# A key of its own for one memset, and one SBUF copy moved ahead of a weight load, in a fused attention + SwiGLU layer

## The chip, the cores and the metric

The kernel runs on one NeuronCore of one Trainium2 chip. Five instruction streams run side by side and meet only through semaphores: TensorE (PE in the profile, with its weight loads listed apart as PEld), VectorE (DVE), ScalarE (ACT), GpSimd (POOL) and SyncE (SP). SP does no arithmetic here; it issues DMAs, in order, and an instruction that waits holds back all that stands behind it on the same engine. The metric is the device time of one execution in microseconds (us), as the median of several; lower is better. Before the change the median of 3 executions is 597.41 us (596.99 to 597.79).

## The reference

One transformer layer in the parallel form: attention and MLP both read the same normalized input and are summed with the residual. S = 2048 tokens, D = 576, 32 heads of 18, a sliding window of 256 tokens, F = 4608, bfloat16.

```
xn  = layernorm(x)
q, k, v = split(xn @ wqkv)                          # 32 heads of 18
p   = softmax(mask(q k^T * 18^-0.5))                # key within the last 256 tokens
h   = silu(xn @ w1) * (xn @ w3)
out = x + concat_heads(p v) @ wo + h @ w2
```

## The kernel before

The tokens are worked in four chunks of 512 (`NC`, four blocks of 128 tokens each, `TB`). For each chunk the kernel needs the normalized input transposed (`xnT`, features on the partitions, 576 features padded to five blocks of 128), then q and k ("QK tiles", nine matmul groups of five), then v, then 36 MLP units (`NF`), between which the attention scores, exponentials and p v products of that chunk are threaded, and last the output projection (`p2_list`), beside which the QK and v tiles of the next chunk are computed. So chunk 0 alone has a prologue in which nothing of the MLP runs; the change lies there.

**Order and waits.** The program is a flat list. Each `add(engine, ..., r=, w=, j=)` appends one instruction to its engine and names keys: `r` reads a key, `w` starts a new generation of it, and `j` joins the writers of the present generation. A reader depends on every writer that the key has *at the moment the reader is added*. `resolve` (line 99) turns the dependencies into semaphore waits and leaves out those that the engine already knows to be met, directly or through another wait. Nothing reorders the list afterwards: the order in which the Python code calls `add` is the order on each engine.

**The prologue, in the order of the code.**

- Four blocks of x are loaded (`load_x`), then the v columns of wqkv into `wa` (lines 681 to 684), key `("wv", n)`.
- The five blocks of 128 features need 640 rows, wqkv has 576. So rows 64 to 127 of the last block of `wa` are cleared by DVE (line 687); this clear starts the key `wz`. Every matmul that reads `wa` reads `wz` too.
- Ten matmuls on zeros (`warm`, line 691).
- SP issues the q and k columns of wqkv (lines 696 and 697, key `wqk`) and then two sets of MLP weights: `load_w13()` twice. One call loads 512 columns of w3 and of w1 into one of three buffers `w13_0`, `w13_1`, `w13_2`, as two DMAs of 576 KB (line 286). A set serves four MLP units.
- For each block: statistics (DVE), rstd (POOL), normalize (DVE), transpose (PE, line 337), copy to `xnT` (ACT, line 331); and one block later its v matmuls (line 371) and their copies (ACT, line 380).
- `xn_swap(0, "sp")` issues two DMAs of 256 KB (line 344) that copy `xnT` into `xnS` with the two halves of the partitions exchanged. The MLP units use the array as two row halves of 64, and `xnS` gives each half the other half's features. The first of the two waits for all of `xnT`. Every MLP unit reads `xnS` as one key.
- ACT gathers the rest of the QK weights into `w8` (line 727).
- POOL clears the q and k buffers `qk`: slots 0 and 1 (line 731), slot 2 (`clear(2)`, line 711), then the padded rows of `wo` (line 733), then slot 3 (`clear(3)`, line 711). The clear of `wo` is added with `j=["wz"]`: it becomes one more writer of the key that the QK weights read.
- `qk_atoms(0, issue_first)` adds the nine QK tiles (line 360, copied to `stage` by DVE, line 364). The first matmul reads `wqk`, `wz` and all of `xnT`. When the tiles of a head group are done, `repack` issues the DMAs (line 414) that spread `stage` into `qk`: groups 0 and 1 right away on SP, the others held back and issued between the MLP units.
- `load_w13()` for the third buffer, then the first of the held groups.

Then the MLP units of chunk 0 begin (line 607, `unit_pairs`): unit 0 reads `xnS` and `w13_0`, unit 1 ends with the first attention scores (line 468), which need group 0 in `qk`, and unit 4 is the first to read `w13_1`.

The output projection reads `wo` in `p2_item` (line 663) with `r=[("oT", tt), "wo", "wz"]`, for the first time at 144.6 us of the profiled execution.

Of the kernel before, what the change touches and what calls it, by code (L numbers as in the profile page):

```python
# [5 lines left out]
dt = mybir.dt  # L6
# [38 lines left out]
class _Prog:  # L45
# [13 lines left out]
    def add(self, eng, fn, r=(), w=(), j=(), dma=None, after=()):  # L59
        deps = []  # L60
        for k in r:
            deps += self.bufs[k].writers
        for k in w:
            g = self.bufs.get(k)
            if g is not None:
                deps += g.ahead(eng)
        for k in j:
            g = self.bufs[k].before
            if g is not None:
                deps += g.ahead(eng)  # L70
        op = _Op(eng, fn, deps + list(after), dma)
        op.after = tuple(after)
        self.n[eng] += 1
        op.pos = self.n[eng]
        if dma is not None:
            self.dma_count[dma] = self.dma_count.get(dma, 0) + 16
            op.cnt = self.dma_count[dma]
        for k in r:
            self.bufs[k].readers.append(op)
        for k in w:  # L80
            self.bufs[k] = _Gen([op], self.bufs.get(k))
        for k in j:
            self.bufs[k].writers.append(op)
        for k in w:
            if self.bufs[k].before is not None:
                self.bufs[k].before.before = None
        self.ops.append(op)
        return op
# [76 lines left out]
def bass_parallel_sum__sliding_block__glu_gated_swiglu__prompt_kernel(  # L165
# [30 lines left out]
    add = P.add  # L196

    with ExitStack() as es:

        def sb(name, shape, dtype=dt.bfloat16):  # L200
            return es.enter_context(nc.sbuf_tensor(name, shape, dtype))
# [14 lines left out]
        wo = sb("wo", [128, 5, D])  # L216
# [22 lines left out]
        oT = sb("oT", [128, TB, 5, 128])  # L239
# [38 lines left out]
        def load_w13():  # L278
            nonlocal nfill
            if nfill >= NC * NFC:  # L280
                return
            s = nfill % NW13
            c0 = (nfill % NFC) * 512
            nfill += 1
            for n, src in enumerate((B_w3, B_w1)):
                add("sp", lambda e, n=n, src=src: e.dma_start(
                    w13[s][64 * n:64 * n + 64, :, :], src[:, c0:c0 + 512].rearrange("(kd p) f -> p kd f", p=64)),
                    dma=f"w13_{s}", **{"j" if n else "w": [("w13", s)]})
# [3 lines left out]
        def load_w2():  # L292
            nonlocal n2fill
            if n2fill >= NC * 2 * NFC:
                return
            s = n2fill % NW2
            half, fc = divmod(n2fill % (2 * NFC), NFC)
            n2fill += 1
            add("sp", lambda e: e.dma_start(
                w2[s][:], B_w2[fc * 512:(fc + 1) * 512, half * HD:(half + 1) * HD].rearrange("(fl p) d -> p fl d", p=128)),  # L300
                w=[("w2", s)], dma=f"w2_{s}")
# [39 lines left out]
        def xn_swap(c, eng):  # L341
            for n in range(2):
                p, q = 64 * n, 64 - 64 * n
                add(eng, lambda e, p=p, q=q: e.dma_start(
                    xnS[p:p + 64, :, :], xnT[q:q + 64, c % 2, 0:4, :]),
                    r=xk(c), dma="xnS", **{"j" if n else "w": ["xnS"]})

        def xk(c):
            return [("xnT", c % 2, tt) for tt in range(TB)]
# [16 lines left out]
        def v_half(c, tt, half, evac):  # L366
            b = ring()
            slot = (c * TB + tt) % (2 * TB)
            c0 = 2 * D + half * HD
            for kd in range(5):  # L370
                add("pe", lambda e, kd=kd: e.matmul(  # L371
                    PS[:, b, 0:HD], xnT[:, c % 2, kd, tt * 128:(tt + 1) * 128], wa[:, kd, c0:c0 + HD],
                    start=(kd == 0), stop=(kd == 4)),
                    r=[("wv", half), "wz", ("xnT", c % 2, tt)], **{"w" if kd == 0 else "j": [("ps", b)]})
            vv = va[:, slot, :, :].rearrange("p g (hh c) -> p (g hh) c", c=VW)
            dst = vv[:, 16 * half:16 * half + 16, 0:Dh]
            src = PS[:, b, 0:HD].rearrange("p (h d) -> p h d", d=Dh)
            kw = {"w" if half == 0 else "j": [("va", slot)]}
            if evac == "act":
                add("act", lambda e: e.activation(dst, src, ACT.Copy), r=[("ps", b)], **kw)  # L380
            else:
                add("dve", lambda e: e.tensor_copy(dst, src), r=[("ps", b)], **kw)
# [266 lines left out]
        def p2_item(c, item, xs):  # L649
            nonlocal of_ctr  # L650
            what, half, fc, k, tt, sl, last = item
            d0 = half * HD
            bank = PS[:, ACC[tt], 0:HD]
            key = [("ps", ACC[tt])]
            if what == "w2":
                f = fc * 4 + k
                add("pe", lambda e: e.matmul(  # L657
                    bank, hT[:, f, tt * 128:(tt + 1) * 128], w2[sl][:, k, :], start=(f == 0), stop=False),
                    r=[("h", f), ("w2", sl)], **{"w" if f == 0 else "j": key})
                if last:  # L660
                    load_w2()
            elif what == "wo":
                add("pe", lambda e: e.matmul(  # L663
                    bank, oT[:, tt, k, :], wo[:, k, d0:d0 + HD], start=False, stop=(k == 4)),
                    r=[("oT", tt), "wo", "wz"], j=key)
            else:
                o = of_ctr % NOF
                of_ctr += 1
                t = c * TB + tt
                add("dve", lambda e: e.tensor_tensor(ofin[o][:], bank, xp[xs[tt]][:, d0:d0 + HD], ALU.add),  # L670
                    r=key + [("xp", xs[tt])], w=[("of", o)])
                add("sp", lambda e: e.dma_start(out2[t * 128:(t + 1) * 128, d0:d0 + HD], ofin[o][:]),
                    r=[("of", o)], dma=f"out{o}")
# [5 lines left out]
        for n, eng in enumerate(("sp", "act")):  # L679
# [3 lines left out]
                w=[("wv", n)], dma=f"wv{n}")  # L683
# [13 lines left out]
        add("sp", lambda e: e.dma_start(  # L697
            wa[:, 0:4, 0:2 * D], A_wqkv[0:512, 0:2 * D].rearrange("(kd p) f -> p kd f", p=128)), j=["wqk"], dma="wqk")
        load_w13()
        load_w13()  # L700

        vall = va[:, :, :, :].rearrange("p t g (hh c) -> p (t g hh) c", c=VW)
        add("pool", lambda e: e.memset(vall[:, :, Dh:VW], 0.0), w=[("va", i) for i in range(2 * TB)])
# [2 lines left out]
        def first_v(tt):  # L706
            v_half(0, tt, 0, "act")
            v_half(0, tt, 1, "act")

        def clear(slot, keys):  # L710
            add("pool", lambda e: e.memset(qk[:, slot, :, :].bitcast(dt.float32), 0.0), w=keys)
# [3 lines left out]
        for i in range(TB):  # L715
# [7 lines left out]
            if i:  # L723
                first_v(i - 1)
        xn_swap(0, "sp")
        first_v(TB - 1)
        add("act", lambda e: e.activation(
            w8[:, :, :].rearrange("p k (s f) -> p k s f", s=2),
            wa[:, :, 0:2 * D].rearrange("p k (s f) -> p k s f", s=2)[:, :, :, 512:576], ACT.Copy),
            r=["wqk", "wz"], w=["w8"])  # L730
        add("pool", lambda e: e.memset(qk[:, 0:2, :, :].bitcast(dt.float32), 0.0), r=[("xn", 1)], w=[("q", g) for g in range(G)])
        clear(2, [("k", g, 0) for g in range(G)])
        add("pool", lambda e: e.memset(wo[0:64, 4, :].bitcast(dt.float32), 0.0), j=["wz"])
        clear(3, [("k", g, 1) for g in range(G)])

        held = []
# [12 lines left out]
        for c in range(NC):  # L749
# [84 lines left out]
            for n, item in enumerate(p2_list(c)):  # L834
                p2_item(c, item, xs)
                if n in late:
                    what, g = late[n]
                    if what == "pv":
                        pv(c, g, ring())
                        pv_out(g)  # L840
                    else:
                        heads_back(g, ring())
                        heads_out(g)
                elif n in ot_at:
                    o_trans(ot_at[n])
                elif n % 8 == 4 and n > 24:
                    next(proj, None)
# [33 lines left out]
```

## Time and profile before

| | us |
|---|---|
| median of 3 executions | 597.41 (596.99 to 597.79) |
| the profiled execution: its own time | 598.63 |
| the profiled execution: span from the first to the last instruction | 596.9 |
| PE busy | 588.9 (99% of the span) |
| DVE / ACT / POOL busy | 327.7 / 264.8 / 170.1 |
| mean granted TensorE clock over the span | 0.997 |

The busy share of an engine counts the time in which it has an instruction under way; for PE this is no measure of how well the array is used. Times of day below ("at 16.43") are microseconds from the start of the span. The timeline gives for each row the start, the time from the first start to the last end, the engine (SPq is SP's issuing of DMAs), the line, the operation, the tiles written and read, the shape and the count; a bracket tells the idle time of the engine before it and what ended it. The chain of waits is the path that ended last, followed back from the last instruction; "issue" in it is time in which the engine waited for nothing that the profile can name. The busy table by stretches gives busy time and count of instructions of each engine, the clock granted to TensorE (1.00 is full), the share of the DMA engines' time in use (it can be read a little above 1), and their rate in GB/s.

### The profile page before, as it was taken

What the parts mean: (1) busy time and instruction counts of PE and PEld (TensorE: products, weight loads), DVE (VectorE), ACT (ScalarE), POOL (GpSimd) and SP (SyncE); (2) the same over time, 40 slices, a digit from 0 to 9 for tenths busy, and PEclk for the clock granted to TensorE, in tenths of its full rate; (3) what the DMA queues carried; (4) which work ended last, traced back from release to release, by engine and by line L of the source; (5) the groups of instructions that cost most, each with busy time, mean ns of one, the idle gap of its engine ahead of it and who ended that gap; (6) DMA issues with size and microseconds to landing.
All of it is one profiled execution on the core that took longest, in us unless ns stands there. A gap on an engine that the chain in (4) does not pass through costs nothing.

```text
span 596.9 us, 14277 instructions
## 1 busy us (share of the span) xinstructions
PE 588.9 (99%) x6300; PEld 373.1 (63%) x6310; DVE 327.7 (55%) x586; ACT 264.8 (44%) x278; POOL 170.1 (28%) x285
## 2 busy tenths in 40 slices
PE   7899999999999999999999999999999999999998
PEld 4355566667765566566775555656677555555776
DVE  4467887644037778654404778765430566666311
ACT  5066666400038687730005778681000677787000
POOL 6133444200015455420002545441000344444000
PEclk9899999999999999999999999999999999999999
DMA  9798989674536757686462858588446366550452
GB/s 238 149 180 167 193 169 195 136 164 126 149 108 124 137 117 134 150 154 147 112 171 75 161 99 154 96 184 161 122 122 168 81 115 128 113 121 1 102 150 68
DMA packets 99041, 81.17 MB, mean 136 GB/s; under 512 B 5028, under 2 KB 97892, under 8 KB 98980
## 3 DMA queue, kind: packets, MB, share of 16 engines
q1 hardware_dynamic: 93065, 74.53, 58.3%
q10 hardware_dynamic: 5915, 5.74, 4.0%
q8 instruction: 49, 0.80, 0.6%
q14 instruction: 12, 0.10, 0.1%
HBM read 71.07 MB, written 2.36 MB: 123 GB/s over the span
## 4 chain that ended last, share of the span: by engine, by line
PE 98%; DVE 1%; issue 1%; DMA 0%; POOL 0%
PE ps L607 48%; PE ps L657 24%; PE ps L360 7%; PE ps L468 6%; PE ps L514 4%; PE ps L663 3%; PE ps L371 3%; PE ps L540 1%; PE ps L589 1%; DMA xp<-in_A_x_dram 0%; DVE xn L319 0%; PE ps L337 0%; PE ps L591 0%; PE ps L530 0%; DVE stats L307 0%
## 5 line engine op out<-in xcount | busy, mean ns | idle before, releaser
L607 PE MATMUL ps<-xnT,w 64*128 64x512 bf16 x1440 | 218.6, 376 | 0.0
L615 ACT ACTIVATE th<-ps 128x512 bf16<-128x512 f32 x144 | 86.0, 597 | 259.2 <-PE ps L607 259.2
L495 POOL TENSOR_SCALAR_AFFINE_SELECT pt<-pt 128x512 bf16<-128x512 bf16 x174 | 107.4, 643 | 186.7 <-ACT pt L484 186.7
L657 PE MATMUL ps<-w,hT 128*128 128x288 bf16 x1152 | 157.7, 286 | 0.0
L607 PE MATMUL ps<-xnS,w 64*128 64x512 bf16 x1152 | 154.1, 376 | 0.0
L621 DVE SCALAR_TENSOR_TENSOR gs<-th,ps 128x512 bf16<-128x512 bf16 x144 | 98.7, 685 | 95.6 <-ACT th L615 95.5
L657 PEld LDWEIGHTS ps<-w,hT 128*128 128x128 bf16 x1152 | 111.9, 98 | 34.8 <-issue 2.3
L484 ACT ACTIVATE pt<-ps 128x1536 bf16<-128x1536 f32 x87 | 126.2, 1451 | 15.2 <-PE ps L468 13.8
L607 PEld LDWEIGHTS ps<-xnT,w 64*128 64x128 bf16 x1440 | 88.2, 94 | 40.2 <-issue 3.3
L624 DVE SCALAR_TENSOR_TENSOR hT<-gs,ps 128x512 bf16<-128x512 bf16 x144 | 98.9, 687 | 5.0
L607 PEld LDWEIGHTS ps<-xnS,w 64*128 64x128 bf16 x1152 | 66.7, 94 | 54.2
L468 PE MATMUL ps<-qk 64*128 64x128 bf16 (+2 forms) x888 | 88.6, 250 | 0.0
L495 POOL TENSOR_SCALAR_AFFINE_SELECT stage<-stage 128x512 bf16<-128x512 bf16 x66 | 40.5, 639 | 155.8 <-ACT stage L484 155.8
L468 PEld LDWEIGHTS ps<-qk 64*128 64x128 bf16 x888 | 48.5, 94 | 31.7 <-ACT pt L484 14.4
L670 DVE TENSOR_TENSOR ofin<-ps,xp 128x288 bf16<-128x288 f32 x32 | 14.6, 456 | 81.8 <-PE ps L663 81.7
L484 ACT ACTIVATE stage<-ps 128x1536 bf16<-128x1536 f32 x33 | 47.9, 1451 | 5.6 <-PE ps L468 5.1
L364 DVE CAST stage<-ps 128x512 bf16<-128x512 f32 x36 | 24.9, 691 | 38.7 <-PE ps L360 38.7
L360 PE MATMUL ps<-xnT,wa 128*128 128x512 bf16 x150 | 39.1, 393 | 3.1 <-issue 2.6
L360 PEld LDWEIGHTS ps<-xnT,wa 128*128 128x128 bf16 x160 | 16.0, 101 | 17.8 <-issue 5.0
L663 PE MATMUL ps<-wo,oT 128*128 128x288 bf16 x160 | 25.3, 286 | 0.0
L523 DVE CAST uT<-ps 128x512 bf16<-128x512 f32 x32 | 21.9, 683 | 5.0 <-PE ps L514 5.0
L371 PE MATMUL ps<-wa,xnT 128*128 128x288 bf16 x160 | 24.0, 286 | 0.0
(51 smaller groups left out, 260.2 us busy)
## 6 DMA issues: line engine op xcount, KB each, us to landing
w<-in_B_w_dram SPq DMA_DIRECT2D x72, 576.0 KB, 7.8
w<-in_B_w_dram SPq DMA_DIRECT2D x72, 288.0 KB, 3.2
xp<-in_A_x_dram SPq DMA_DIRECT2D x30, 144.0 KB, 7.2
qk<-stage ACTq DMA_DIRECT2D x75, 36.0 KB
out_dram<-ofin SPq DMA_DIRECT2D x32, 72.0 KB, 1.8
xnS<-xnT ACTq DMA_DIRECT2D x6, 256.0 KB, 5.4
wa<-in_A_wqkv_dram SPq DMA_DIRECT2D x1, 1152.0 KB, 8.8
qk<-stage SPq DMA_DIRECT2D x25, 36.0 KB
```

The source lines that it names most:

```text
L360: add("pe", lambda e, kd=kd, ws=ws: e.matmul(PS[:, b, :], ws, xnT[:, c % 2, kd, :], start=(kd == 0), stop=(kd == 4)), r=["w8" if i == 8 el ...
L364: add("dve", lambda e: e.tensor_copy(stage[:, i, :], PS[:, b, :]), r=[("ps", b)], w=st_keys(i))
L371: add("pe", lambda e, kd=kd: e.matmul(PS[:, b, 0:HD], xnT[:, c % 2, kd, tt * 128:(tt + 1) * 128], wa[:, kd, c0:c0 + HD], start=(kd == 0), ...
L468: return add("pe", lambda e: e.matmul(SC[:, col:col + n], qk[r0:r0 + 64, 2 + kc % 2, g, kt * 128:(kt + 1) * 128], qk[r0:r0 + 64, h % 2, g, ...
L484: add("act", lambda e: e.activation(pt_slot(sl).rearrange("p h q -> p (h q)"), SC, ACT.Exp, scale=scale), r=[("ps", b) for b in (5, 6, 7)] ...
L495: add("pool", lambda e, vb=vb, edge=edge: e.affine_select(out=vb, in_=vb, compare_op=ALU.is_ge, fill=0.0, base=-1 if edge else 0, pattern= ...
L607: add("pe", lambda e, n=n, r0=r0, r=r, k=k, src=src: e.matmul(PS[:, b0 + r, :], w13[sl][r0:r0 + 64, k, fl * 128:(fl + 1) * 128], src, star ...
L615: add("act", lambda e: e.activation(th[i][:], PS[:, bg, :], ACT.Tanh, scale=0.5), r=[("ps", bg)], w=[("th", i)])
L621: add("dve", lambda e: e.scalar_tensor_tensor(out=gs[i][:], in0=th[i][:], scalar=1.0, in1=PS[:, bg, :], op0=ALU.add, op1=ALU.mult), r=[("t ...
L624: add("dve", lambda e: e.scalar_tensor_tensor(out=hT[:, u, :], in0=gs[i][:], scalar=0.5, in1=PS[:, bu, :], op0=ALU.mult, op1=ALU.mult), r= ...
L657: add("pe", lambda e: e.matmul(bank, hT[:, f, tt * 128:(tt + 1) * 128], w2[sl][:, k, :], start=(f == 0), stop=False), r=[("h", f), ("w2", ...
L663: add("pe", lambda e: e.matmul(bank, oT[:, tt, k, :], wo[:, k, d0:d0 + HD], start=False, stop=(k == 4)), r=[("oT", tt), "wo", "wz"], j=key)
```

## The change

Two edits. The clear of `wo`'s padded rows starts a key `woz` of its own, and the output projection reads `woz` in place of `wz`. And the second `load_w13()` of the prologue, the one that fills `w13_1`, is called after `xn_swap(0, "sp")` in place of before it, so that on SP the two `xnS` DMAs stand ahead of the two DMAs of `w13_1`.

```diff
             elif what == "wo":
                 add("pe", lambda e: e.matmul(
                     bank, oT[:, tt, k, :], wo[:, k, d0:d0 + HD], start=False, stop=(k == 4)),
-                    r=[("oT", tt), "wo", "wz"], j=key)
+                    r=[("oT", tt), "wo", "woz"], j=key)
...
             wa[:, 0:4, 0:2 * D], A_wqkv[0:512, 0:2 * D].rearrange("(kd p) f -> p kd f", p=128)), j=["wqk"], dma="wqk")
-        load_w13()
         load_w13()
...
         xn_swap(0, "sp")
+        load_w13()
         first_v(TB - 1)
...
-        add("pool", lambda e: e.memset(wo[0:64, 4, :].bitcast(dt.float32), 0.0), j=["wz"])
+        add("pool", lambda e: e.memset(wo[0:64, 4, :].bitcast(dt.float32), 0.0), w=["woz"])
```

Between the two programs as built, three things differ. On PE the first QK matmul waits for the semaphores of ACT and of the `wqk` load, and no longer for POOL's. On SP the two `xnS` DMAs come before the two of `w13_1`. And on SP the first `repack` DMA now waits for POOL (the clears of `qk`) as well as for DVE. The order on PE, DVE, ACT and POOL is the same.

## The prediction

> **What bounds the kernel now.** I read the page's engine shares first, then PE's waits over the whole run, then the chain of waits and the timeline where PE stands still, last the landings of the transfers around that place. Engine shares, and the waits of PE over the run (total, times, longest):
>
> ```profile
> PE 588.9 (99%) x6300; PEld 373.1 (63%) x6310; DVE 327.7 (55%) x586; ACT 264.8 (44%) x278; POOL 170.1 (28%) x285
> ```
> ```profile
> PE ps L360 <- issue: 2.6, 1, 2.6
> PE ps L691 <- DVE uT L686: 1.2, 1, 1.2
> PE ps L337 <- DVE xn L319: 0.9, 2, 0.8
> ```
>
> PE is the bound, and after its first matmul it stands still for longer than a microsecond once only: 2.6 us before the first QK matmul (L360). No other wait of PE in the run reaches this list after that, so whatever moves this place forward moves the end, unless something later is not ready in time. The chain of waits from 13 to 32 us (start, duration, what):
>
> ```profile
> 12.96 0.86 PE ps L371 x7
> 13.82 2.61 issue
> 16.43 11.35 PE ps L360 x44
> 27.78 3.99 PE ps L607 x36
> 31.77 0.33 PE ps L468 x3
> ```
>
> The profile calls the gap "issue", that is, it names no releaser. The waits in the program do: ACT, POOL and the `wqk` load. The v copy that last used the first tile's bank ended at 12.44 (ACT, 12.02 + 0.42), the last `xnT` block at 12.14, and `wqk`, issued at 3.40 with 8.8 us to its landing, is there at 12.2. POOL is left:
>
> ```profile
> 10.59 3.51 POOL L731 MEMSET qk<- 128x4096 f32 x1 [0.74 <-DVE xn L319]
> 14.04 1.80 POOL L711 MEMSET qk<- 128x2048 f32 x1
> 15.79 0.33 POOL L733 MEMSET wo<- 64x288 f32 x1
> ```
>
> The clear of `wo` is third in a queue of clears and ends at 16.12; PE's weight load starts at 16.18 and the matmul at 16.43. The reader is to see that a 0.33 us memset that QK does not need holds it for 2.61 us. The clock, by stretches (PE busy and count, PEld, DVE, ACT, POOL, clock, DMA share, GB/s):
>
> ```profile
> 9.69:13.10 3.41, 3.41 (x35) 2.79 (x32) 0.64 (x2) 2.96 (x7) 2.67 (x2) 1.00 1.12 232
> 13.10:16.51 3.41, 0.80 (x7) 0.54 (x7) 0.00 (x0) 1.45 (x3) 3.41 (x4) 1.00 1.14 206
> 16.52:19.93 3.41, 3.41 (x9) 1.23 (x9) 0.69 (x1) 0.00 (x0) 1.34 (x1) 0.50 1.14 212
> 19.93:23.34 3.41, 3.41 (x18) 1.51 (x16) 2.07 (x3) 0.00 (x0) 0.00 (x0) 1.00 1.12 223
> ```
>
> Right after the stretch in which PE was mostly idle (0.80 of 3.41 us busy) the granted clock is 0.50 for 3.41 us: 9 matmuls where the next stretch has 18. The gap costs twice, once as idle time and once as a slow restart.
>
> **The change part by part.** *The new key.* It removes PE's wait on POOL. The next conditions for the first QK matmul are those above, all met by 12.44; later tiles need banks freed by ACT at 13.04, 13.65 and 14.27, before PE gets to them (1.08 us a tile). So QK follows the v matmuls at 13.82; I allow 0.1 for the hand-over. Without the gap the stretch 13.10 to 16.51 is busy, and I expect no drop of the clock. The casts of two late tiles start at 22.42 and 23.50, so a tile takes 1.08 us and nine take 9.72, against 11.35 in the chain: the slow restart costs 1.63. QK ends at 13.92 + 9.72 = 23.64 and not at 27.78: a gain of 4.14 on the path, 2.51 from the gap and 1.63 from the clock. The clear itself still runs on POOL. The output projection's new key costs nothing: its first matmul comes at 144.6, the clear ends at 16.12, and PE has waited for later POOL work by then.
>
> The clock term has two ends. A gain of 1.63 is what this one execution shows. [...] A stretch with 0.80 of 3.41 busy was followed by the slow clock, and 6.28 to 9.69, with 3.10 busy, was not; where the limit lies between is not shown. I take 1.63, the only measured row, and keep zero for the range.
>
> [...]
>
> *The moved copy.* MLP unit 0 now wants `xnS` and `w13_0` at 23.64. Of SP's queue, the issue times and the landings before, by the row of each line in a narrow window:
>
> ```profile
> 4.03 6.08 SPq L286 DMA_DIRECT2D w<-in_B_w_dram  x4
> 12.16 2.39 SPq L344 DMA_DIRECT2D xnS<-xnT  x2
> 20.98 7.39 SPq L414 DMA_DIRECT2D qk<-stage  x9
> 28.41 1.36 SPq L286 DMA_DIRECT2D w<-in_B_w_dram  x2
> ```
>
> The four weight DMAs, issued at 4.03, 4.72, 5.42 and 6.10, land 11.0, 13.2, 15.4 and 17.5 us later: at 15.0, 17.9, 20.8 and 23.6, one every 2.87 us. The two copies, issued at 12.16 and 13.95, land 12.2 and 11.9 us later, at 24.3 and 25.8. Transfers of this queue land in order, at a rate that the DMA engines set. Left where it was, the copy would land 2.2 us after PE wants it. Moved ahead of `w13_1` it stands behind `w13_0` alone (17.9). Its own two landings came 2.27 us after the last weights (23.58 to 25.85), so I put it at 17.9 + 2.3 = 20.2; the other end is 25.8, no gain at all. I take 20.2, since order in the queue is what the rows show. PE waits for neither, with 3.4 us to spare.
>
> What the copy passes pays. The copy still waits for ACT until 12.14, and behind it on SP stand both `w13_1` DMAs and all repacks. Two issues at 0.60 and two at 0.64 bring SP to 14.7; even with the 1.75 us that the first copy took before, to 15.8. The `w13_1` landings slip by the copy's 2.3 us to about 25.9. PE first reads that set at 36.52, after the change at about 32.4: 6.5 us to spare.
>
> *SP's new wait and the first scores.* The first repack now waits for POOL's clear of slot 2, done at 15.84, and for DVE's second cast: 13.92 + 2.16 + 0.69 = 16.8. DVE comes last, so the wait on POOL costs nothing. The four DMAs of group 0 took SP from 20.98 to 24.47, now 16.8 to 20.3. Unit 1 reads them at 31.60, now at about 27.5. On the queue they stand behind `w13_1` (25.9) and carry 4 x 36 KB, 0.7 us at 200 GB/s: about 26.6, 0.9 us to spare. This is the tightest place. Bounds: the outputs' 1.8 us from issue to landing (page) would give 22.1, the 12.2 us that the copy took before would give 32.5, a stall of 5.0. I take 26.6; the DMA share falls from 1.11 at 22 to 0.44 at 24 us before, so the queue is nearly empty by then.
>
> Behind that, repacks, the third weight set and the refills are set off by DVE and PE and shift with them.
>
> **Sum.** Against the profiled execution: 598.63 - 4.14 = 594.5. Its time is 1.22 above the median shown (597.41), for a reason that the profile does not tell; I carry the difference over: 597.41 - 4.14 = 593.3.
>
> **Rivals.** (B) The gap goes, but the usual execution had little of the slow clock to lose: gain 2.5, time 594.9. For it: the median is 1.22 below the profiled time. Against: 3 executions within 0.8 us.
> (C) Group 0 lands a little late, up to 1.5 us of stall: 593.3 to 594.8. For it: only 0.9 us to spare, and landing times worked out to about 1 us.
> (D) The copy is no earlier, 25.8: a stall of 2.2, time 595.5. Against: the landings in order.
> (E) Another wait takes POOL's place before QK, say ACT or `wqk`: nothing gained, 597.4. Against: all are done by 12.44.
> (F) Slower: the repacks of group 0 take as long as the copy did behind the weights, 12.2 us from the last issue, and land at 32.5. PE stands 5.0 us in unit 1, in order, with everything behind it; net +0.9, time 598.3. It decides once group 0 lands later than 31.6; it passes 0.2% at 32.8. Against: the copy was issued with weights ahead of it that went on landing for another 11.4 us (12.16 to 23.6), group 0 with 5.6 us of them at most (20.3 to 25.9).
>
> **How the numbers follow.** Chances: the forecast 0.52, B 0.25, C 0.10, D 0.04, E 0.05, F 0.04. The forecast's own range is 592.5 to 594.2 (the executions' 0.8 us around 593.3). Taking in B with some scatter and most of C and D, the range is 592.4 to 595.6, which leaves out E, F and the tails. About 0.2% (1.2 us) can be told from no change. Faster by more: forecast, B, C and D, 0.91. Within: E and half of F, which fits 0.06. Slower: 0.03.
>
> **What would show it.** In the changed profile PE has no gap before L360, which starts near 13.9, and the clock is 1.00 from 16 to 20 us; right if QK's chain row is about 9.7 us. `xnS` lands near 20, `w13_1` near 26, and L607 starts near 23.6. The first L468 comes near 27.5 with no wait before it. Wrong if PE idles before L607 (the copy) or before the first L468 (group 0), or if the clock is at 0.50 after 16 us all the same.

## The result, and the profile after

The changed kernel takes 595.9 us (median of 8 executions, 594.35 to 596.51) against 597.6 us before (8 executions, 596.93 to 599.66). The ratio is 0.9959, with a 95% interval of 0.9943 to 0.9976: 0.41% or 2.4 us faster by the ratio. The forecast was 593.3 us, 4.1 us faster than 597.41. Taken from 597.41 by the ratio, the time after is 595.0 us, inside the range of 592.4 to 595.6, near its upper end; the 595.9 us as they stand lie above it, since the kernel before took 597.6 in these runs.

The profiled execution after took 595.91 us, its span is 594.2. The waits of PE over the run (who, for what: total, times, longest):

```profile
PE ps L337 <- DVE xn L319: 1.5, 2, 1.3
PE ps L691 <- DVE uT L686: 1.2, 1, 1.2
PE ps L371 <- DMA wa<-in_A_wqkv_dram: 0.6, 1, 0.6
PE ps L360 <- DMA wa<-in_A_wqkv_dram: 0.5, 1, 0.5
```

The 2.6 us named "issue" before L360 are gone. In their place stands a wait of 0.5 us on the q and k weights, and the v matmuls (L371) wait 0.6 us for theirs. The chain of waits around the place (start, duration, what):

```profile
3.40 11.66 DMA wa<-in_A_wqkv_dram
15.05 0.05 issue
15.10 9.89 PE ps L360 x45
24.99 3.99 PE ps L607 x36
28.98 0.33 PE ps L468 x3
```

The load of the q and k weights, issued at 3.40 as before, lands at 15.05 where the profile of before had it at 12.2. QK starts at 15.10; the forecast had 13.92. The stretches after the old gap (PE busy and count, then PEld, DVE, ACT, POOL, clock, DMA share, GB/s):

```profile
13.10:16.51 3.41, 2.88 (x19) 1.64 (x18) 0.12 (x1) 2.05 (x5) 3.41 (x4) 1.00 1.13 206
16.52:19.93 3.41, 3.41 (x18) 1.54 (x16) 2.25 (x4) 0.00 (x0) 1.32 (x1) 1.00 1.08 232
```

The clock stays at 1.00 and 18 matmuls fit where 9 did. SP's queue of the changed kernel shows the new order:

```profile
4.03 1.57 SPq L286 DMA_DIRECT2D w<-in_B_w_dram  x2
12.91 1.17 SPq L344 DMA_DIRECT2D xnS<-xnT  x2
14.12 1.84 SPq L286 DMA_DIRECT2D w<-in_B_w_dram  x2
18.19 7.38 SPq L414 DMA_DIRECT2D qk<-stage  x9
```

The second copy, issued at 13.47, lands 9.2 us later, at 22.7, ahead of the 24.99 at which the MLP begins. So the two edits did what they say; the gain is smaller for two reasons that the experiments below separate: a load that had been hidden came last, and the profile read for the forecast was not the usual execution of the kernel before.

One observation holds everything together. From the start of the MLP (the first L607 of the chain) to the end of the span, the time hardly changes: 596.9 - 27.78 = 569.1 before, 594.2 - 24.99 = 569.2 after, and 568.8 to 569.5 in every other profile of this study but two, which wait once more after that start. Whatever decides the start of the MLP decides the time.

### The profile page after: what moved, and what is told of

Its sections match the earlier page's. It is cut to its first block, busy times and chain, and to the rows that moved or that the text cites. A ratio compares the mean times of both kernels' runs of the same rounds, so it can differ in the third digit from the quotient of the medians.

```text
span 594.2 us, 14288 instructions
## 1 busy us (share of the span) xinstructions
PE 587.6 (99%) x6310; PEld 372.7 (63%) x6310; DVE 328.0 (55%) x586; ACT 264.9 (45%) x278; POOL 169.8 (29%) x285
## 4 chain that ended last, share of the span: by engine, by line
PE 97%; DMA 2%; SPq 0%; DVE 0%; issue 0%
PE ps L607 49%; PE ps L657 24%; PE ps L360 7%; PE ps L468 6%; PE ps L514 4%; PE ps L663 3%; PE ps L371 2%; DMA wa<-in_A_wqkv_dram 2%; PE ps L540 1%; PE ps L589 1%; PE ps L591 0%; PE ps L530 0%; SPq L273 0%; SPq L696 0%; SPq L684 0%; DVE ofin L670 0%
## 5 line engine op out<-in xcount | busy, mean ns | idle before, releaser
L607 PE MATMUL ps<-xnT,w 64*128 64x512 bf16 x1440 | 218.7, 377 | 0.0
L607 PE MATMUL ps<-xnS,w 64*128 64x512 bf16 x1152 | 154.2, 377 | 0.0
L484 ACT ACTIVATE pt<-ps 128x1536 bf16<-128x1536 f32 x87 | 126.2, 1450 | 15.2 <-PE ps L468 13.8
L607 PEld LDWEIGHTS ps<-xnT,w 64*128 64x128 bf16 x1440 | 88.3, 94 | 40.2 <-issue 3.3
L607 PEld LDWEIGHTS ps<-xnS,w 64*128 64x128 bf16 x1152 | 66.7, 94 | 54.1
L360 PE MATMUL ps<-xnT,wa 128*128 128x512 bf16 x160 | 38.6, 379 | 0.5 <-DMA wa<-in_A_wqkv_dram 0.5
L360 PEld LDWEIGHTS ps<-xnT,wa 128*128 128x128 bf16 x160 | 15.6, 98 | 14.7 <-DMA wa<-in_A_wqkv_dram 0.8
L371 PE MATMUL ps<-wa,xnT 128*128 128x288 bf16 x160 | 24.1, 286 | 0.6 <-DMA wa<-in_A_wqkv_dram 0.6
## 6 DMA issues: line engine op xcount, KB each, us to landing
wa<-in_A_wqkv_dram SPq DMA_DIRECT2D x1, 1152.0 KB, 11.7
```

The lines of the kernel that those rows point to most:

```text
L360: add("pe", lambda e, kd=kd, ws=ws: e.matmul(PS[:, b, :], ws, xnT[:, c % 2, kd, :], start=(kd == 0), stop=(kd == 4)), r=["w8" if i == 8 el ...
L371: add("pe", lambda e, kd=kd: e.matmul(PS[:, b, 0:HD], xnT[:, c % 2, kd, tt * 128:(tt + 1) * 128], wa[:, kd, c0:c0 + HD], start=(kd == 0), ...
L484: add("act", lambda e: e.activation(pt_slot(sl).rearrange("p h q -> p (h q)"), SC, ACT.Exp, scale=scale), r=[("ps", b) for b in (5, 6, 7)] ...
L607: add("pe", lambda e, n=n, r0=r0, r=r, k=k, src=src: e.matmul(PS[:, b0 + r, :], w13[sl][r0:r0 + 64, k, fl * 128:(fl + 1) * 128], src, star ...
```

## The experiments

Each kernel was run beside runs of the kernel before on the same chip, and ratios are against those.

**The new key alone.**

```diff
-                    r=[("oT", tt), "wo", "wz"], j=key)
+                    r=[("oT", tt), "wo", "woz"], j=key)
...
-        add("pool", lambda e: e.memset(wo[0:64, 4, :].bitcast(dt.float32), 0.0), j=["wz"])
+        add("pool", lambda e: e.memset(wo[0:64, 4, :].bitcast(dt.float32), 0.0), w=["woz"])
```

> The new key alone, the second weight set still ahead of the copy. Theory: PE leaves the v matmuls for QK without the POOL wait, and QK ends near 23.6 us, or near 25.0 where the q and k weights land late, as they did at 15.05 us in the profile of the change. The copy lands near 25.8 us as before, so PE stands 2.2 us (0.8 us) before the first MLP matmul, which starts near 25.9 in every execution. Gain over before 1.9 us, the same for early and late landings, so less scatter than the full change. A rival says that the moved weight set itself is what delays the q and k weights: then they land here at 12.2 us in every execution, and QK starts at 13.9. Another rival says that the copy lands earlier than the rows of before let expect: then the gain is that of the full change.

598.49 us against 597.94: ratio 1.0014 (1.0002 to 1.0026), slightly slower, where a gain of 1.9 us was expected. Its chain of waits:

```profile
3.40 12.21 DMA wa<-in_A_wqkv_dram
15.60 0.04 issue
15.65 9.89 PE ps L360 x45
25.54 2.02 issue
27.56 4.06 PE ps L607 x36
```

PE leaves POOL's clear behind and then stands 2.02 us before the MLP: the second copy, behind both weight sets, lands at 27.5. The stall of 2.2 us in the expectation is what came; the gain did not, because the MLP starts where it started before. The q and k weights land at 15.6 with the second weight set queued early as in the kernel before, so they come late without that set being moved, and the rival that moving it is what delays them is out.

Five of the 11 executions have a mean clock of 0.997, with a median of 599.19 us; the six at 1.000 have 598.23, against 597.86 for the executions of the kernel before at full clock on this chip. That is the largest share of any kernel here. Which idle time goes with them, the 1.0 us before QK or the 2.0 before the MLP, is not shown: the profiled execution has no drop.

**The moved copy alone.**

```diff
-        load_w13()
         load_w13()
...
         xn_swap(0, "sp")
+        load_w13()
```

> The moved copy alone, with POOL's clear still in the key. Theory: PE starts QK at 16.4 us as before, the copy lands near 20 to 23 us, before QK's end, and no time is gained: ratio 1.000, within 0.2%. The landing of the q and k weights is then visible in the profile and invisible in the time, whether it is 12 or 15 us. Rival (moving the weights delays the q and k weights): they land near 15 us here, and near 12 in the kernel with the key alone.

596.57 us against 597.94, ratio 0.9984 (0.9975 to 0.9993): 1.0 us faster by the ratio, where none was expected. Its chain:

```profile
3.40 10.82 DMA wa<-in_A_wqkv_dram
14.22 2.05 issue
16.28 9.87 PE ps L360 x45
26.15 3.99 PE ps L607 x36
```

POOL still holds QK to 16.28, but there is no wait before the MLP, which starts at 26.15. So in the kernel before, the copy must come last in many executions, though the first profile shows no such wait. Ten of the 11 executions lie within 596.37 to 596.92, all at a mean clock of 1.000. The eleventh, at 0.997, took 598.25: 1.68 us above the median. That is what a drop of the clock cost here, where nothing hides it; it is one execution. The ten others lie within 0.55 us, the closest of all kernels run here: POOL's clears alone set the start, and they end at nearly the same time in the three profiles in which QK waits for them alone (QK from 16.43, 16.20 and 16.28).

**Filling the gap.**

```diff
         first_v(TB - 1)
+        warm(SPARE, 10)
         add("act", lambda e: e.activation(
```

> The kernel before with ten more matmuls on zeros (2.2 us at full clock) between the v matmuls and QK; the output is unaffected and POOL's wait stays. It measures the clock term by itself. Theory: the first QK matmul starts at 16.4 us as before, the granted clock stays at 1.00, QK takes 9.7 us and not 11.35: 1.6 us faster than before. Rival (the usual execution had nothing to lose to the clock): same time as before, within 0.3 us. If the time is 0.8 us faster or so, some executions lost it and others did not.

598.12 us against 597.94, ratio 0.9998 (0.9985 to 1.0012). None of the 11 executions shows a clock below 1.000, and nothing is gained. In the profile QK takes 9.71 us, as expected without a drop, and then PE waits:

```profile
14.43 2.16 PE ps L691 x10
16.59 9.71 PE ps L360 x45
26.30 0.87 issue
27.17 4.06 PE ps L607 x36
```

The wait before the MLP is at the same place as with the key alone, 0.87 us and not 2.02; the profile names no releaser. Of the 63 executions of the kernel before that ran beside the experiments, 13 have a mean clock of 0.997. Their median is 598.8 us, that of the other 50 is 597.9: most executions lose nothing to the clock, and those that do are 0.9 us slower, less than the 1.68 of the moved copy.

**The kernel before, once more.**

> The kernel before once more, for a second profile of it. Theory formed from the first four runs: the profile that the prediction was read from was not the usual execution. In the usual one the clock stays at 1.00, the q and k weights land at 14 to 15.6 us (hidden, since POOL holds QK to 16.2), QK ends at 26.0, and PE then stands 0.5 to 1.7 us until the second half of the copy lands, near 27 us. Rival: it looks like the first profile again, with the clock at 0.50 from 16.5 us, weights at 12.2 and no wait before the first MLP matmul.

597.75 us, span 596.0, clock 1.00. The chain:

```profile
13.02 2.45 PE ps L371 x20
15.47 0.73 issue
16.20 9.87 PE ps L360 x45
26.07 1.05 issue
27.11 4.06 PE ps L607 x36
```

This is another execution than the one that the forecast was read from. The wait on POOL is 0.73 us and not 2.61, since the v matmuls end at 15.47 (PE ran slowly for longer at the start: the four matmuls on zeros take 1.71 us, 1.03 in the first profile); QK takes 9.87 and not 11.35; and a wait of 1.05 us stands before the MLP, until the second copy lands at 27.0. The q and k weights, 11.3 us on their way, land at 14.7, unseen behind POOL. The two profiles of the kernel before start the MLP 0.67 us apart (27.78 and 27.11), by different sums. The long slow start is itself not usual, 2 of the 14 profiles of this study have it; but behind POOL's clears it moves nothing that shows, and the filled gap, without it, starts the MLP at 27.17.

**The full change, again,** with no edit, on the chip of the next experiments:

> The full change once more, on the chip of the next two. Theory: median near 595.9, with executions between 594.3 (weights land before the v matmuls are done) and 596.5 (they land at 15 us or later); profile with a wait on the q and k weights before QK of 0 to 1.3 us and no wait before the first MLP matmul.

595.52 us against 597.93, ratio 0.9956 (0.994 to 0.9972), 594.13 to 596.21. In the profile QK waits 0.9 us for its weights, which land at 15.1, and nothing before the MLP.

**The q and k weights in two parts,** on top of the full change.

```diff
-        add("sp", lambda e: e.dma_start(wa[0:64, 4, 0:2 * D], A_wqkv[512:576, 0:2 * D]), w=["wqk"], dma="wqk")
-        add("sp", lambda e: e.dma_start(
-            wa[:, 0:4, 0:2 * D], A_wqkv[0:512, 0:2 * D].rearrange("(kd p) f -> p kd f", p=128)), j=["wqk"], dma="wqk")
+        add("sp", lambda e: e.dma_start(wa[0:64, 4, 0:2 * D], A_wqkv[512:576, 0:2 * D]), w=["wqk0"], dma="wqk0")
+        for n, (f0, f1) in enumerate(((0, 256), (256, D))):
+            for s in range(2):
+                add("sp", lambda e, c0=s * D + f0, c1=s * D + f1: e.dma_start(
+                    wa[:, 0:4, c0:c1], A_wqkv[0:512, c0:c1].rearrange("(kd p) f -> p kd f", p=128)),
+                    dma=f"wqk{n}", **{"w" if n and not s else "j": [f"wqk{n}"]})
...
-                    r=["w8" if i == 8 else "wqk", "wz"] + xk(c), **{"w" if kd == 0 else "j": [("ps", b)]})
+                    r=["w8" if i == 8 else f"wqk{i % 4 // 2}", "wz"] + xk(c), **{"w" if kd == 0 else "j": [("ps", b)]})
...
-            r=["wqk", "wz"], w=["w8"])
+            r=["wqk0", "wqk1", "wz"], w=["w8"])
```

> The full change, with the q and k weights loaded in two parts: columns 0 to 255 of q and of k first, the rest after, each with its own key, so the first four QK tiles wait for 44% of the bytes. Theory (in the usual execution of the change QK waits for a late landing of these weights): the 0.5 us gap before QK goes in such executions, and the median is 0.3 to 0.6 us below that of the change, about 595.4. Rival (the executions differ in something else, the clock or the start): no difference from the change, 595.9. If the smaller rows (512 bytes) slow the loads, the second part may hold the fifth tile.

595.17 us, ratio 0.9955 (0.9941 to 0.9968). The profiled execution (span 592.0) has no wait before QK, which starts at 13.46. Run again beside the full change:

> The full change with the q and k weights in two parts, once more. Theory: QK's first wait is gone, so the median is 0.3 to 1.0 us below the full change on the same chip, and what scatter is left comes from the v weights and from the second part. Rival: the late landing was not what held the full change; then the two medians agree within 0.2 us.

594.66 against 595.52 for the full change on that chip; ratios to before 0.9943 (0.9925 to 0.9961) and 0.9956. The medians differ as expected, but the intervals overlap, so a gain from the split is possible and not shown; its first run, at 0.9955, gives none. Its profile names what comes last once QK no longer waits (PE's waits):

```profile
PE ps L337 <- DVE xn L319: 1.7, 2, 1.5
PE ps L691 <- DVE uT L686: 1.2, 1, 1.2
PE ps L468 <- DMA qk<-stage: 0.9, 1, 0.9
```

The first scores wait 0.9 us for the repack of group 0, which lands at 28.5, behind the second weight set (27.2). This was the tightest place of the forecast, put at 26.6.

**The v weights in longer rows,** on top of the split: one DMA of 1152-byte rows on SP and the tail on ACT, in place of two of 576-byte rows and two tails.

```diff
-        for n, eng in enumerate(("sp", "act")):
-            c0 = 2 * D + n * HD
...
+        add("act", lambda e: e.dma_start(
+            wa[0:64, 4, 2 * D:3 * D], A_wqkv[512:576, 2 * D:3 * D]), w=[("wv", 0)], dma="wv0")
+        add("sp", lambda e: e.dma_start(
+            wa[:, 0:4, 2 * D:3 * D], A_wqkv[0:512, 2 * D:3 * D].rearrange("(kd p) f -> p kd f", p=128)),
+            w=[("wv", 1)], dma="wv1")
```

> The same, and the v weights loaded as rows of 1152 bytes in one DMA on SP and the padded tail in one on ACT, in place of rows of 576 bytes in two on each queue: half the packets ahead of the q and k weights. Theory (what is late in the prologue is late because the DMA engines work through packets in order): the v weights land before PE wants them at 8 us, everything behind them comes a little earlier, and the time is 0.2 to 0.8 us below the split alone. Rival (packet count is not what delays them): same time as the split.

595.46 us, ratio 0.9956 (0.9939 to 0.9973): not faster than the split. PE does not wait for the v weights, but group 0 lands at 28.86, no earlier than in the split (28.47), and holds PE for 1.3 us. That fewer rows ahead bring in earlier what stands behind them is not shown, nor that the DMA engines work through packets in order, as the expectation's theory has it; one profile of each cannot exclude it either.

**The second weight set issued after group 0's repack,** on the split and on the full change.

```diff
         xn_swap(0, "sp")
-        load_w13()
...
                 repack(c, g, "sp")
+                if g == 0:
+                    load_w13()
```

> The q and k weights in two parts, and the second MLP weight set issued after the four repack DMAs of head group 0 in place of ahead of them. Theory: in the split, what came last was group 0, landing at 28.5 us because it stood behind that weight set (27.2); now it lands by 23 to 25 us, PE does not wait before the first scores, and QK starts right after the v matmuls: span 592.3 to 592.8 in nearly every execution, 594.2 us, 0.5 to 1.0 below the split's 594.7 to 595.2. The second set lands near 29 us and is wanted near 32. Rival (group 0's landing is its own long path, not the queue ahead): PE still waits about 1 us there and the time is the split's.

595.57 us against 598.8 on this chip, ratio 0.9952 (0.9939 to 0.9964). The wait before the first scores is gone, as expected; the median is not the 594.2 expected, nor below the split's. In the profiled execution, which at 595.08 is faster than the median, the v weights come last (landing at 8.5, a wait of 0.3 us, QK from 14.23); what held the slower ones is not shown.

> The full change with the same later issue of the second MLP weight set, the q and k weights in one part. Theory: group 0 is not what came last in the full change (its profiles show a wait on the q and k weights, none before the scores), so the late executions stay late and the median is that of the full change, 595.5 to 595.9, scatter 594.2 to 596.4. Rival (the second weight set, issued from 12.9 us on, slows the q and k weights): they land before 14 us and the median falls to 594.3.

595.63 us, ratio 0.9953 (0.9938 to 0.9968): the full change's ratio, as expected. The q and k weights land at 13.8, within what the other profiles show, and the v weights hold PE twice (0.6 us in sum).

**All three.** The split, the longer v rows and the later weight set, beside the full change for a third time.

> Three edits on top of the full change: q and k weights in two parts, v weights in one DMA of 1152-byte rows and a tail, and the second MLP weight set issued after the repack of head group 0. Theory: each of the waits that came last in one of the profiles is then gone (q and k weights, group 0, v weights); PE has no wait longer than 0.3 us between the first v matmul and the MLP, span 592.4 to 593.2 in most executions, and the median is 0.8 to 1.5 us below the full change on the same chip. Rival (something common to all of them, the input rows and the statistics ahead of the v matmuls, scatters by as much): median within 0.4 us of the full change.

> The full change on the same chip, for the comparison. Theory: median 595.5 to 596.0, scatter 594.2 to 596.5, and in its profile the q and k weights land at 14 to 15.5 us with a wait of up to 1 us before QK.

594.68 us against 598.62, ratio 0.994 (0.9927 to 0.9953); the full change on that chip 595.32, ratio 0.9954 (0.9937 to 0.9971). It has the lowest ratio of all the kernels (executions from 594.4 to 595.7), but its interval overlaps the full change's, so that it beats it is not shown. The difference of 0.64 us lies between what was expected (0.8 to 1.5) and the rival (up to 0.4). Its own profiled execution was its slowest (595.70): PE has no wait longer than 0.3 us between the first v matmul and the MLP, as expected, but it shows a third thing that scatters, how long PE runs slowly at the very start:

```profile
7.12 1.71 PE ps L689 x4
8.82 0.53 PE ps L337 x5
9.36 1.57 PE ps L371 x10
```

The four matmuls on zeros take 1.71 us, 0.43 each, where the first profile of before has them in 1.03, and the v matmuls are late by that. At full clock such a matmul takes 0.22 (ten in 2.16 us in the filled gap). In the first profiles of before and of after the clock column reads 1.00 over this place (1.24 to 7.8 us), so the slow start is read from the length of the matmuls alone, and the mean clock of an execution does not show it.

The third profile of the full change is the execution that the forecast described:

```profile
11.33 2.45 PE ps L371 x20
13.78 0.05 issue
13.83 9.66 PE ps L360 x44
23.49 3.99 PE ps L607 x36
27.48 0.33 PE ps L468 x3
```

The q and k weights land at 12.3 here, not at 14 to 15.5 as expected. QK follows the v matmuls without a wait, the MLP starts at 23.49, the span is 592.7. The forecast's were 13.92, 23.64 and 596.9 - 4.14 = 592.8. Its own time is 594.38 us, where the forecast's first sum, 598.63 - 4.14, gave 594.5.

## Why the prediction was right, and where it was not

The direction held, both waits are gone, and by the ratio the time is in the range; the size did not hold.

**The new key: right in kind.** PE no longer waits for POOL, the clear of `wo` runs where it ran, and QK takes 9.7 to 9.9 us at full clock. SP's new wait on POOL cost nothing visible: in the profile after, the repacks start at 18.19, right behind DVE's second cast (17.47 + 0.69).

**"`wqk` ... is there at 12.2": the step that failed first.** That was read from one execution and used as a condition met by 12.44. The landings in nine profiles with this load in one piece are 12.2, 14.7 (before), 15.05, 15.1, 12.3 (after), 15.6 (key alone), 14.2 (move alone), 14.5 (filled gap) and 13.8 (later weight set), always issued at 3.40. Before, POOL held QK to 16.2 and hid all of them. After, the load is last in two of the three profiles of the full change. The forecast's rival E named this wait, and put it at the whole gain. In the first profile after, QK starts 1.2 us later than forecast (15.10 against 13.92): 0.5 us of it is this wait, and the rest the v weights, which came late as well (0.6 us).

**The clock term: a price that not every execution pays.** The forecast took 1.63 us as "the only measured row" and kept zero for the range. The price is near the 1.68 of the one execution of the moved copy that paid it, but only 13 of 63 executions of the kernel before have the drop. The profiled execution of 598.63 was one of them, which is a reason for its 1.22 us above the median that the forecast did not find. So 598.63 - 4.14 = 594.5 fits the like execution after (594.38), while 597.41 - 4.14 took a gain of 1.63 off a median that for the most part does not hold it. Zero was the right end. No run shows why an execution loses nothing; that 50 of the 63 have no such drop is what was measured.

When the clock drops is not settled. After PE's idle time of 2.61 us in the first profile it was 0.50 for 3.41 us; after idle times of 2.13 us (move alone), 2.02 us (key alone) and 0.73 us (second profile of before) it stayed at 1.00. What decides between them no run shows, nor what idle time the other executions with a drop had.

**The copy: the term that was missing.** For the moved copy the forecast had no gain of its own; it saw only that the copy would be late once QK was early (2.2 us; measured 2.02 with the key alone, where QK's end and the landing both came 1.6 to 1.9 us later than forecast, so that the agreement is partly luck). In an execution at full clock it was late already: a wait of 1.05 us in the second profile of before, 0.87 at the same place in the filled gap, and a ratio of 0.9984 for the move alone. Its place after the change was put at 20.2; it landed at 22.7, 22.9 and 19.9, before QK's end each time. "Transfers of this queue land in order", from which its place was worked out, holds in the first profile and not in the profile after: there the first copy lands at 18.7, ahead of the second DMA of `w13_0` at 20.3, which was issued 8.2 us earlier. `w13_1`, put at 25.9, landed at 26.9 in the profile after, and PE waits for it in none of the three profiles of the full change.

**The sum, redone from executions at full clock.** From the second profile of before to the first after: QK starts at 15.10 and not at 16.20 (1.1 us), and the wait of 1.05 us before the MLP is gone; together 2.1, which is the move of the MLP's start from 27.11 to 24.99. The median's 2.4 us is near that. Rival B's time, 594.9, comes nearest, and its reason (little of the slow clock to lose) is right, but its 2.51 us of gap is not what was gained: that number agrees by chance. Neither edit alone is worth the sum: key alone 1.0014, move alone 0.9984, both 0.9959. POOL, the copy and the weights stood side by side, and each hid the next.

**What stays open.** Why the q and k weights land anywhere between 12.2 and 15.6 us. It is not the second weight set behind them (key alone: 15.6 with it queued early; later weight set: 13.8 without it), and the v weights in half the rows ahead of them gave no gain that shows. Part of the delay is there before this load: the 144 KB of the same weights that SP issues just ahead of it, at 2.77, land 5.4 us later in the first profile of before (this load at 12.2) and 6.9 us later in the first after (15.05). What causes it no run here tells.

## What to carry to other kernels

Where several transfers and engines meet at one start, the waits show only the one that came last (a landing at 14.7 stood in no wait of PE here, behind clears that held it to 16.2); before pricing the removal of a wait, read the landing of everything else that the same instruction, and the next stage, needs, and treat a margin no larger than the scatter of the landings as none (the same load scattered by 3.4 us here). A single profile fixes the price of an event such as a drop of the clock, not how often it happens: the mean clock of the other executions tells that, so ask for it, or for a second profile, before adding the price to a median. Two edits that remove two waits on the same start have to be made together to be measured (ratios 1.0014 and 0.9984 alone, 0.9959 together).

## What was not expected of the hardware

A load of 1152 KB, issued at the same 3.40 us in the same program, took 11.7, 11.7 and 8.9 us to land in three profiles of the full change and 8.8 and 11.3 in two of the kernel before. A mean clock of 0.997, which in the first profile comes from one drop, appears in some executions of a kernel and not in others: 13 of 63 before, 5 of 11 with the key alone, 1 of 11 with the moved copy alone, 0 of 11 with the gap filled, 1 of 23 with the full change; the idle time that a drop followed is known for that profile alone (2.61 us). And the slow matmuls at the very start of the kernel, 0.43 us each and not 0.22, with the clock column at 1.00 in the first profiles of before and of after, end earlier or later from one execution to the next, which alone moved the end of the v matmuls by 1.65 us (13.82 and 15.47 in the two profiles of the kernel before).
